# Issuing the W_in sums a step before their splits, and three smaller moves, in a fused attention and two-MLP kernel

## The chip, the cores and the metric

One core of a Trainium2 chip. The metric is the device time of one launch in microseconds (us), as a median of runs. The engines have short names in the profile: PE is TensorE (PEld its weight loads), DVE is VectorE, ACT is ScalarE, POOL is GpSimd, SP is the queue that issues the DMAs.

## The reference

```python
def _attn_ref(q, k, v, p):            # q, k, v (8, 8, 576, 64), p (8, 8, 32, 64)
    p_packed = sm_attn(p, k, v)       # softmax(p k^T / 8) v
    return sm_attn(q, p_packed, p_packed)
def _moe_ref(x, w_in, w_out):         # x (4608, 512), w_in (512, 2048), w_out (2048, 512)
    h = x @ w_in
    return (h - np.tanh(h)) @ w_out
def _moe2_ref(x, w_in, w_out):        # the same sizes
    h = x @ w_in
    return (h * np.cos(h)) @ w_out
# out = moe2(moe(attention, heads side by side))
```

## The kernel before

All large matrix products are done in a split form: a float32 operand is written as a high part, rounded to the format that TensorE takes (`hi`), and the rest (`lo`), and three products hi·hi, lo·hi and hi·lo are added in PSUM. ScalarE makes each high part, VectorE or GpSimd the low part by a subtraction.

The work stands in three stages.

**Stage A, the first MLP** (with attention worked in between): 128 steps, `n` from 0 to 127. A step takes one block of 288 tokens and 256 of the 2048 hidden columns: `h1` (12 matmuls, L454), `el1` and `el2` (tanh by two branches on ScalarE and VectorE; the choice between them is the COPY_PREDICATED of L488), `el3` (`gh`, L496) and `el4` (`gl`, L501), and two steps later `ymm1` (24 matmuls, L516), which adds to four PSUM tiles `y`. After the last step of a block `yevac1` (L552) has ScalarE copy the four tiles out, behind the `ymm1` of that step and so two steps after its `h1`. The next block's first `ymm1` writes the same four tiles. In the last 16 steps (n = 112 to 127) the weights of the second MLP are converted as well, ten of the 32 tiles. A conversion has three parts: `a` on ScalarE (L135), `b`, three VectorE instructions (L147, L152, L157) that stand between the ones of `el2` a step later, and `c`, a ScalarE copy (L180) and a GpSimd subtraction (L181), another step later. How many `a` a step gets is `STEP_A2`, indexed by n − 112.

**Stage B, the second MLP for three blocks of 512 tokens**: 24 steps, `n` from 0 to 23, in five parts (`PARTS`): tokens 0, steps of columns 0 to 3; tokens 1, columns 0 to 3; tokens 2, columns 0 to 7; tokens 0, columns 4 to 7; tokens 1, columns 4 to 7. A step is `h2` (24 matmuls, L580), the chain `el_cos` (ScalarE L602, VectorE L605, ScalarE L611 and L612, VectorE L615, ScalarE L621 which makes `gh`, VectorE L624 which makes `gl`), and then the y products of the step before (24 matmuls, L637, in `chunks`). So `gh` of step n is wanted when `h2` of step n + 1 is done. The other 22 conversions stand in steps 0 to 10. In the last steps but one of a part, `splity` splits the activations of the next part (ScalarE L568, GpSimd L569, four tiles, two a step): in steps 13, 14 for part 3 and in steps 17, 18 for part 4. From step 12 on `combine(F)` makes four sums of quarters of W_in for the third stage: six GpSimd instructions (L691, L694, four of L702), a ScalarE copy (L704), a VectorE subtraction (L705), two stores. F is 0, 1, 2, 3 in steps 12 to 15, 4 and 5 in step 16, 6 and 7 in step 17. `combine` takes two of the three buffers of the tag "st". From step 19 on `bprep` makes the activations' sums for stage C: 40 small pieces, spread over steps 19 to 23; pieces 1 and 21 are loads into "st" buffers.

**Stage C, the second MLP for the other six blocks, in three pairs**: seven products (`prod`, L783) in place of eight, from the sums. `load_wa` loads the weight sums of one F, `load_wo` those of W_out.

From step 15 of stage A on the order is written out by hand: each engine carries out its instructions in the order of the program, and waits where an operand or a buffer isn't there. A ScalarE instruction that waits holds up all that stand behind it on ScalarE. The DMAs are all issued on one queue (SP), in program order too. At the end of a step of stage B the order on ScalarE is: `gh`, the two copies of `splity`, the copies out of PSUM where a part ends, then the copy of L704; then the next step's L602.

Of the kernel before, what the change touches and what calls it, by code (L numbers as in the profile page):

```python
# [34 lines left out]
PRE_A = (0, 1, 1, 1, 1, 0, 1, 1, 1, 0, 1, 1, 0, 0, 0)  # L35
PRE_B = (1, 0, 1, 1, 2, 0, 2, 2, 0, 1, 2, 2, 0, 3, 0)
STEP_A = (1, 2, 2, 2, 1, 2, 1, 1, 1, 1, 0, 2, 1, 1, 1, 1, 1, 1, 0, 3, 1, 1)
STEP_A2 = (1, 1, 0, 1, 1, 0, 1, 1, 0, 1, 1, 0, 1, 1, 0, 0)
STEP_ORDERED = 15
ATT1 = ((-2, 0, 1, 4), (0, 1, 2, 5))  # L40
ATT = ((0, 2, 3, 8), (1, 4, 5, 10))
# [4 lines left out]
YLOAD, Y2LOAD, Y2SPLIT = 2, 118, 125  # L46
PARTS = ((0, 0, 4), (1, 0, 4), (2, 0, 8), (0, 4, 8), (1, 4, 8))
NCL, CONVS, BPREP = 3, 12, 19
COMBINE = {12: (0,), 13: (1,), 14: (2,), 15: (3,), 16: (4, 5), 17: (6, 7)}
SGN = -2147483648  # L50


# [1 line left out]
def fused_kernel(ctx, tc, qT, kT, v, pT, w1i, w1o, w2i, w2o, ident, out):  # L54
    nc = tc.nc
# [33 lines left out]
    def f32(ap):  # L89
        return ap.bitcast(F32)  # L90

    def wtile(name):
        return wp.tile([128, 2, 512], F32R, tag="w", name=name)
# [7 lines left out]
    class Conv:  # L101
# [69 lines left out]
        def b(self):  # L171
            for fn in self.b_ops():
                fn()
# [389 lines left out]
    def splity(i, yr, eng):  # L563
        if i % 2 == 0:
            t = a2p.tile([128, 2, S], F32R, tag="a2", bufs=4, name="yhl")[:, :, 0:TB]
        else:
            t = p3.tile([128, 2, TB], F32R, tag="yhl", bufs=4, name="yhl")
        nc.scalar.activation(out=t[:, 0, :], in_=yr, func=AF.Copy)  # L568
        eng.tensor_tensor(out=t[:, 1, :], in0=yr, in1=f32(t[:, 0, :]), op=ALU.subtract)  # L569
        return t  # L570

    def h2(s, yt, st):
        h = pss("h")
        for x in range(2):
            f = 2 * s + x
            conv2.need(w2in, f)
            n = 0
            for wa, ya in ((0, 0), (1, 0), (0, 1)):
                for k in range(4):
                    nc.tensor.matmul(  # L580
                        out=h[:, x, :], lhsT=w2in[f][:, wa, 128 * k:128 * k + 128],
                        rhs=yt[k][:, ya, :], start=(n == 0), stop=(n == 11),
                    )
                    n += 1
        st["h"] = h
# [100 lines left out]
    def combine(F):  # L686
        r = p2x["r"]
        f0, f1 = w2in[2 * F], w2in[2 * F + 1]
        w = r.tile([128, 2, 512], F32, tag="st", bufs=3, name="cw")
        c = r.tile([128, 4, 256], F32, tag="st", bufs=3, name="cs")  # L690
        nc.gpsimd.tensor_tensor(  # L691
            out=w[:, 0, :], in0=f32(f0[:, 0, :]), in1=f32(f0[:, 1, :]), op=ALU.add
        )
        nc.gpsimd.tensor_tensor(  # L694
            out=w[:, 1, :], in0=f32(f1[:, 0, :]), in1=f32(f1[:, 1, :]), op=ALU.add
        )
        a11, a12, a21, a22 = (w[:, i // 2, 256 * (i % 2):256 * (i % 2) + 256] for i in range(4))
        for i, (x, y, op) in enumerate((
            (a21, a22, ALU.add), (c[:, 0], a11, ALU.subtract),
            (a11, a21, ALU.subtract), (a12, c[:, 1], ALU.subtract),  # L700
        )):
            nc.gpsimd.tensor_tensor(out=c[:, i], in0=x, in1=y, op=op)  # L702
        hi, lo = (wp.tile([128, 4, 256], F32R, tag="w", name="ws") for _ in range(2))
        nc.scalar.activation(out=hi, in_=c, func=AF.Copy)  # L704
        nc.vector.tensor_tensor(out=lo, in0=c, in1=f32(hi), op=ALU.subtract)  # L705
        nc.sync.dma_start(out=wsd[F][:, 0], in_=f32(hi.rearrange("p c n -> p (c n)")))
        nc.sync.dma_start(out=wsd[F][:, 1], in_=f32(lo.rearrange("p c n -> p (c n)")))

    def load_wa(F):
        t = [wtile("wa") for _ in range(4)]  # L710
        nc.sync.dma_start(out=f32(t[2]), in_=wid[2 * F])
        for i in range(2):
            nc.sync.dma_start(out=f32(t[i].rearrange("p a n -> p (a n)")), in_=wsd[F][:, i])
        nc.sync.dma_start(out=f32(t[3][:, :, 256:512]), in_=wid[2 * F + 1][:, :, 256:512])
        sh, sl = (x.rearrange("p a n -> p (a n)") for x in t[:2])

        def combo(i):
            return [(sh, sl)[wa][:, 256 * i:256 * i + 256] for wa in range(2)]

        return {  # L720
            "S1": combo(0), "S2": combo(1), "S3": combo(2), "S4": combo(3),
            "A11": [t[2][:, wa, 0:256] for wa in range(2)],
            "A12": [t[2][:, wa, 256:512] for wa in range(2)],
            "A22": [t[3][:, wa, 256:512] for wa in range(2)],
        }
# [7 lines left out]
    def bprep(t, bo):  # L733
        ops, q = [], {}

        def split(n, j, src):
            d = bo.setdefault(n, [None, None])

            def hi():
                d[j] = wtile("b")  # L740
                nc.scalar.activation(out=d[j][:, 0, :], in_=src(), func=AF.Copy)

            def lo():
                nc.vector.tensor_tensor(
                    out=d[j][:, 1, :], in0=src(), in1=f32(d[j][:, 0, :]), op=ALU.subtract
                )

            return [hi, lo]

        def sub(o, a, b):  # L750
            return lambda: nc.vector.tensor_tensor(out=o(), in0=a(), in1=b(), op=ALU.subtract)

        for j in range(2):
            def load(j=j):
                for n, k in (("lo", j), ("hi", 2 + j)):
                    q[n, j] = p2x["r"].tile([128, 2, TB], F32, tag="st", bufs=3, name="yq")
                    nc.sync.dma_start(
                        out=q[n, j],
                        in_=y1[k, :, t * TB:t * TB + 2 * TB].rearrange("p (a n) -> p a n", a=2),
                    )  # L760

            def temp(j=j):
                q["t", j] = p2x["r"].tile([128, 2, TB], F32, tag="st", bufs=3, name="yt")

            b11, b12 = (lambda j=j, i=i: q["lo", j][:, i] for i in range(2))
            b21, b22 = (lambda j=j, i=i: q["hi", j][:, i] for i in range(2))
            t1, t2 = (lambda j=j, i=i: q["t", j][:, i] for i in range(2))
            s11, s1, s2 = split("B11", j, b11), split("T1", j, t1), split("T2", j, t2)
            s3, s21, s22 = split("T3", j, b12), split("B21", j, b21), split("B22", j, b22)
            s4 = split("T4", j, b21)  # L770
            ops += [
                load, temp, s11[0], sub(t1, b12, b11), s11[1], s1[0], sub(t2, b22, t1), s1[1],
                s2[0], sub(b12, b22, b12), s2[1], s21[0], s3[0], s21[1], sub(b21, b21, t2),
                s3[1], s22[0], s4[0], s22[1], s4[1],
            ]
        return ops
# [44 lines left out]
    def run_pool(name, **kw):  # L821
        c = tc.tile_pool(name=name, bufs=1, reuse_waits="tile", **kw)
        return c, c.__enter__()
# [140 lines left out]
    hist, yr0 = [], []  # L964
    steps = [(blk, HS * h + s) for h in range(2) for blk in range(NP) for s in range(HS)]
    steps += [(blk, s) for blk in range(NP, NB) for s in range(NSTEP)]
    for n, (blk, s) in enumerate(steps):
# [17 lines left out]
        if blk >= NB - 2:  # L985
            na = STEP_A2[n - NSTEP * (NB - 2)]
        else:
# [35 lines left out]

    p2c, p2 = run_pool("p2")
    p3c, p3 = run_pool("p3")
    pend, hist, bo, nyt = [], [], {}, []
    seq = [(i, t, s, a, b) for i, (t, a, b) in enumerate(PARTS) for s in range(a, b)]
    nxt = [p[0] for p in PARTS[1:]]

# [5 lines left out]
    for n, (i, t, s, a, b) in enumerate(seq):  # L1035
        st = {}
        if s == a and i:
            yt, nyt = nyt, []
        h2(s, yt, st)
        el_cos(st, 2 if n < CONVS else 0, n == 0)  # L1040
        if i < len(nxt):
            r = s - a - (b - a - 4)
            if r in (1, 2):
                for _ in range(2):
                    nyt.append(splity(i + 1, yr0.pop(0), nc.gpsimd))
            if r in (0, 1):
                yr0 += [loady(nxt[i], k) for k in range(2 * r, 2 * r + 2)]
        if hist:
            flush(*hist.pop(0))
            keep = 2 if n == len(seq) - 1 else 0  # L1050
            while len(pend) > keep:
                pend.pop(0)()
        hist.append((t, s, st, a, b))
        if a and s == b - 2 and n < len(seq) - 2:
            load_op(t)
        store_w2()
        for F in COMBINE.get(n, ()):
            combine(F)
        if n == BPREP:
            prep = bprep(NCL, bo)  # L1060
        if n >= BPREP:
            m = -(-len(prep) // (len(seq) - n))
            for fn in prep[:m]:
                fn()
            prep = prep[m:]
    was = [load_wa(0)]
    flush(*hist.pop(0))
    p3c.__exit__(None, None, None)
    pshc.__exit__(None, None, None)
# [17 lines left out]
    for t in pairs:  # L1087
# [66 lines left out]
        if not last:  # L1154
            bo = {}
            prep = bprep(t + 2, bo)
            was = [load_wa(0)]
        else:
            prep = []
        for F in range(NSTEP):  # L1160
# [4 lines left out]
            n = -(-len(prep) // max(1, 6 - F))  # L1165
            for fn in prep[:n]:
                fn()
            prep = prep[n:]
# [58 lines left out]
```

## Time and profile before

| what | value |
| --- | --- |
| median of 3 runs | 1590.18 us |
| lowest, highest | 1587.25, 1590.53 us |
| the profiled execution, its own time | 1587.97 us |
| span of that execution in the trace | 1586.1 us |
| PE busy | 1497.8 us, 94% |
| DVE busy | 1171.5 us, 74% |
| ACT busy | 900.2 us, 57% |
| POOL busy | 234.5 us, 15% |

Times in rows are counted from the start of the span. In the rows of stretches the first stretch is step 11 of stage B, the second its steps 12 to 19, the third the last 16 steps of stage A. By the matmuls' lines stage A ends at about 795 us, stage B runs from there to about 1078 us, and stage C from 1082 us to the end. The granted clock of TensorE (PEclk) is 1.00 at full speed.

### The profile page before, as it was taken

To read this page: it belongs to the slowest core of one execution; us is meant where nothing else is said; L and a number is where in the kernel's file an instruction comes from. 1 tells how busy PE (TensorE), PEld (TensorE's weight loads), DVE (VectorE), ACT (ScalarE), POOL (GpSimd) and SP (SyncE) were. 2 spreads that over 40 slices of the span, in tenths; PEclk is the share of its full clock that TensorE was granted. 3 is DMA by queue.
4 is the path that set the end of the run, shared out by engine and by line. 5 is a ranking of instruction groups with operands and counts; after the bars stand their busy time and mean duration, and the time that the engine had idled before them with its cause. 6 is when DMAs were issued, how large, how long until landed. Compare 5 with 4: busy or idle time off the path is not lost.

```text
span 1586.1 us, 25956 instructions
## 1 busy us (share of the span) xinstructions
PE 1497.8 (94%) x10192; PEld 1298.0 (82%) x10192; DVE 1171.5 (74%) x1604; ACT 900.2 (57%) x1385; POOL 234.5 (15%) x186
## 2 busy tenths in 40 slices
PE   4789999999999999999899998798999999999999
PEld 1669888999899999998877786687888888888887
DVE  6999988887878788789877853356777477747661
ACT  4768665675756666676656653454555354535541
POOL 3632110010101010011233327500000000000000
PEclk7789999999999999999999999999999999999999
DMA  9423322111212111114446622543757474747542
GB/s 346 152 96 105 98 79 91 64 46 31 59 51 64 61 64 61 32 53 162 136 162 230 226 100 84 196 175 129 266 188 268 147 285 162 261 157 281 189 164 116
DMA packets 88506, 223.54 MB, mean 141 GB/s; under 512 B 8960, under 2 KB 36608, under 8 KB 88384
## 3 DMA queue, kind: packets, MB, share of 16 engines
q1 hardware_dynamic: 88384, 221.88, 40.2%
q8 instruction: 81, 1.33, 0.3%
q14 instruction: 41, 0.34, 0.1%
HBM read 173.34 MB, written 48.50 MB: 140 GB/s over the span
## 4 chain that ended last, share of the span: by engine, by line
PE 68%; DVE 16%; issue 8%; POOL 4%; ACT 3%; DMA 1%; SPq 0%; DVEq 0%; POOLq 0%; ACTq 0%
PE y L516 19%; PE y L637 19%; PE p L783 15%; PE h L454 9%; DVE wt L147 2%; PE h L580 2%; DVE y L484 2%; DVE wt L157 2%; PE gp L416 2%; DVE y L488 1%; POOL cs L702 1%; DVE d L482 1%; DVE wt L152 1%; DVE t L481 1%; DVE gl L501 1%
## 5 line engine op out<-in xcount | busy, mean ns | idle before, releaser
L516 PE MATMUL y<-gh,w1o 128*128 128x288 f32 x2048 | 310.5, 304 | 11.6 <-ACT gh L496 6.7
L516 PEld LDWEIGHTS y<-gh,w1o 128*128 128x128 f32 x2048 | 283.7, 190 | 39.8 <-ACT t L469 14.9
L783 PE MATMUL p<-b,wa 128*128 128x512 f32 x1008 | 241.9, 391 | 4.1 <-issue 4.1
L454 PE MATMUL h<-a,g 128*128 128x288 f32 x1536 | 229.7, 299 | 14.0 <-ACT w1i L135 6.6
L454 PEld LDWEIGHTS h<-a,g 128*128 128x128 f32 x1536 | 214.0, 191 | 18.4 <-ACT w1i L135 7.6
L783 PEld LDWEIGHTS p<-b,wa 128*128 128x128 f32 x1008 | 190.4, 189 | 44.0 <-issue 4.5
L469 ACT ACTIVATE t<-h 128x576 f32<-128x576 f32 x128 | 83.2, 650 | 206.3 <-PE h L454 206.0
L637 PE MATMUL y<-wo,gh 128*128 128x512 f32 x768 | 188.1, 389 | 0.0
L637 PEld LDWEIGHTS y<-wo,gh 128*128 128x128 f32 x768 | 144.2, 188 | 29.9
L516 PE MATMUL y<-gl,w1o 128*128 128x288 f32 x1024 | 159.5, 298 | 1.4 <-DVE gl L501 1.4
L516 PEld LDWEIGHTS y<-gl,w1o 128*128 128x128 f32 x1024 | 145.0, 191 | 1.9 <-DVE gl L501 1.9
L580 PE MATMUL h<-yhl,w2i 128*128 128x512 f32 x576 | 134.9, 390 | 0.8 <-ACT w2i L180 0.6
L481 DVE TENSOR_TENSOR t<-h,t 128x576 f32<-128x576 f32 x128 | 95.2, 744 | 54.3 <-ACT u L470 53.9
L580 PEld LDWEIGHTS h<-yhl,w2i 128*128 128x128 f32 x576 | 108.0, 188 | 23.9 <-ACT w2i L180 1.0
L488 DVE COPY_PREDICATED y<-k,t 128x576 f32<-128x576 int16 x128 | 116.1, 907 | 11.6
L637 PE MATMUL y<-w2o,gh 128*128 128x512 f32 x384 | 99.1, 405 | 18.8 <-ACT gh L621 16.7
L794 ACT ACTIVATE a<-ha 128x1024 f32<-128x1024 f32 x24 | 25.5, 1063 | 145.6 <-DVE ha L791 145.6
L501 DVE TENSOR_TENSOR gl<-y,gh 128x576 fp32r<-128x576 f32 x128 | 102.7, 802 | 6.8 <-ACT gh L496 6.0
L496 ACT ACTIVATE gh<-y 128x576 fp32r<-128x576 f32 x128 | 87.6, 685 | 32.1 <-DVE y L488 30.1
L637 PEld LDWEIGHTS y<-w2o,gh 128*128 128x128 f32 x384 | 74.7, 196 | 37.3 <-ACT gh L621 18.7
L484 DVE SCALAR_TENSOR_TENSOR y<-y,d 128x576 f32<-128x576 f32 x128 | 101.2, 791 | 0.1
L637 PE MATMUL y<-wo,gl 128*128 128x512 f32 x384 | 97.8, 389 | 0.0
(120 smaller groups left out, 2168.4 us busy)
## 6 DMA issues: line engine op xcount, KB each, us to landing
wo<-wod SPq DMA_DIRECT2D x96, 512.0 KB, 6.6
wa<-wsd SPq DMA_DIRECT2D x48, 512.0 KB, 6.2
wa<-wid SPq DMA_DIRECT2D x24, 512.0 KB, 5.6
y<-ye SPq DMA_DIRECT2D x80, 144.0 KB, 1.9
out<-o SPq DMA_DIRECT2D x36, 256.0 KB, 2.2
st<-w1i SPq DMA_DIRECT2D x16, 512.0 KB, 7.2
v<-vv SPq DMA_DIRECT2D x16, 512.0 KB, 4.7
st<-w1o SPq DMA_DIRECT2D x16, 512.0 KB, 6.2
```

Of the source, the lines that this page charges most:

```text
L147: nc.vector.tensor_scalar(out=wi, in0=wi, scalar1=3, scalar2=None, op0=ALU.logical_shift_left)
L454: nc.tensor.matmul(out=h[:, x, 0:HB], lhsT=gw[b, f // 4, half][:, ga, c0:c0 + 128], rhs=a2[b, half][:, aa, HB * j:HB * j + HB], start=(n = ...
L469: nc.scalar.activation(out=st["t"], in_=h, func=AF.Tanh)
L481: lambda: nc.vector.tensor_tensor(out=t, in0=hs, in1=t, op=ALU.subtract),
L484: lambda: nc.vector.scalar_tensor_tensor(out=y, in0=y, scalar=PC0 - PC1 * PC1 / (4 * PC2), in1=d, op0=ALU.add, op1=ALU.mult,),
L488: lambda: nc.vector.copy_predicated(out=y, mask=k.bitcast(I16), data=t),
L496: nc.scalar.activation(out=st["gh"], in_=st["g"], func=AF.Copy)
L501: nc.vector.tensor_tensor(out=st["gl"], in0=st["g"], in1=f32(st["gh"]), op=ALU.subtract)
L516: nc.tensor.matmul(out=yps[blk][d][:, 0:HB], lhsT=w1out[f][:, wh, 128 * d:128 * d + 128], rhs=st[gg][:, x, :], start=(s in first and x == ...
L580: nc.tensor.matmul(out=h[:, x, :], lhsT=w2in[f][:, wa, 128 * k:128 * k + 128], rhs=yt[k][:, ya, :], start=(n == 0), stop=(n == 11),)
L637: nc.tensor.matmul(out=yps[t, lo_s][m], lhsT=st[gg][:, x, 128 * m:128 * m + 128], rhs=w[:, wh, :], start=(s == lo_s and x == 0 and not lo ...
L783: nc.tensor.matmul(out=dst, lhsT=wa[wi][:, 128 * j:128 * j + 128], rhs=b[j][:, bi, :], start=(n == 0), stop=(n == 5),)
```

## The change

`combine` is cut in two: `combine` issues the six GpSimd instructions, and the new `combine2` the ScalarE copy, the VectorE subtraction and the two stores, one step later. The sums are spread as 0 to 5 in steps 11 to 16 and 6 and 7 in step 17, so that `combine2` stands in steps 12 to 17 (one each) and 18 (two). The low parts of `splity` for parts 3 and 4 go from GpSimd to VectorE (eight instructions). The first piece of `bprep`, a load, stands in step 18 in place of 19, and the first `load_wa` of the pairs in step 22 in place of behind step 23. `STEP_A2` has the same ten conversions, otherwise spread: no `a` in steps 113 and 121 (the steps that end with copies out of PSUM), and the last one in step 126 in place of 125.

```diff
-STEP_A2 = (1, 1, 0, 1, 1, 0, 1, 1, 0, 1, 1, 0, 1, 1, 0, 0)
+STEP_A2 = (1, 0, 1, 1, 0, 1, 1, 0, 1, 0, 1, 1, 0, 1, 1, 0)
...
-COMBINE = {12: (0,), 13: (1,), 14: (2,), 15: (3,), 16: (4, 5), 17: (6, 7)}
+COMBINE = {11: (0,), 12: (1,), 13: (2,), 14: (3,), 15: (4,), 16: (5,), 17: (6, 7)}
...
             nc.gpsimd.tensor_tensor(out=c[:, i], in0=x, in1=y, op=op)
+        return F, c
+
+    def combine2(F, c):
         hi, lo = (wp.tile([128, 4, 256], F32R, tag="w", name="ws") for _ in range(2))
         nc.scalar.activation(out=hi, in_=c, func=AF.Copy)
         nc.vector.tensor_tensor(out=lo, in0=c, in1=f32(hi), op=ALU.subtract)
...
-    pend, hist, bo, nyt = [], [], {}, []
+    pend, hist, bo, nyt, sums = [], [], {}, [], []
...
-                    nyt.append(splity(i + 1, yr0.pop(0), nc.gpsimd))
+                    nyt.append(splity(i + 1, yr0.pop(0), nc.gpsimd if i < 2 else nc.vector))
...
-        for F in COMBINE.get(n, ()):
-            combine(F)
-        if n == BPREP:
+        for x in sums:
+            combine2(*x)
+        sums = [combine(F) for F in COMBINE.get(n, ())]
+        if n == BPREP - 1:
             prep = bprep(NCL, bo)
+            prep.pop(0)()
+        if n == len(seq) - 2:
+            was = [load_wa(0)]
         if n >= BPREP:
...
-    was = [load_wa(0)]
     flush(*hist.pop(0))
```

## Rows read from the trace of the kernel before

**Rows 1.** PE's waits, whole span: line, what ended them, us in total, times, longest
```profile
PE y L637 <- ACT gh L621: 16.7, 4, 9.4
PE p L783 <- issue: 4.1, 1, 4.1
```

**Rows 2.** Busy us (x) of PE, PEld, DVE, ACT, POOL; PEclk; DMA, by stretch
```profile
917.69:928.57 10.88, 10.88 (x49) 9.01 (x48) 6.48 (x7) 5.69 (x7) 4.92 (x4) 1.00 0.29 104
928.57:1037.81 109.24, 93.00 (x385) 75.15 (x384) 42.05 (x35) 46.72 (x51) 58.57 (x55) 0.92 0.34 125
...
698.97:795.39 96.42, 88.42 (x627) 86.58 (x625) 87.47 (x116) 65.57 (x117) 17.01 (x12) 0.96 0.42 138
```

**Rows 3.** PE in time, stage B: start, us, instructions, in brackets idle before
```profile
934.01 3.79 PE L637 MATMUL y<-w2o,gh 128*128 128x512 f32 x16
...
969.16 5.53 PE L637 MATMUL y<-w2o,gh 128*128 128x512 f32 x16 [2.35 <-ACT gh L621]
...
986.35 2.05 PE L637 MATMUL y<-w2o,gh 128*128 128x512 f32 x4 [4.40 <-ACT gh L621]
...
1030.51 5.65 PE L637 MATMUL y<-w2o,gh 128*128 128x512 f32 x16 [9.40 <-ACT gh L621]
```

**Rows 4.** ACT in time, steps 13 and 17 of stage B
```profile
945.09 1.03 ACT L602 ACTIVATE a<-h 128x1024 f32<-128x1024 f32 x1 [3.11 <-PE h L580]
...
950.85 1.06 ACT L621 ACTIVATE gh<-a 128x1024 fp32r<-128x1024 f32 x1 [1.29 <-DVE a L615]
...
961.13 1.06 ACT L704 ACTIVATE ws<-cs 128x1024 fp32r<-128x1024 f32 x1 [8.18 <-POOL cs L702]
...
1022.49 1.06 ACT L704 ACTIVATE ws<-cs 128x1024 fp32r<-128x1024 f32 x1 [5.43 <-POOL cs L702]
```

**Rows 5.** POOL in time, step 13 of stage B
```profile
952.50 3.09 POOL L569 TENSOR_TENSOR yhl<-yr,yhl 128x512 fp32r<-128x512 f32 x2 [19.74 <-ACT yhl L568]
...
960.36 0.74 POOL L702 TENSOR_TENSOR cs<-cw,cs 128x256 f32<-128x256 f32 x1
```

**Rows 6.** DVE in time: splits, `gl` beside sums on POOL, `gl` alone
```profile
793.00 1.29 DVE L569 TENSOR_TENSOR yhl<-yr,yhl 128x512 fp32r<-128x512 f32 x2 [1.28 <-ACT yhl L568]
...
986.33 2.11 DVE L624 TENSOR_TENSOR gl<-a,gh 128x1024 fp32r<-128x1024 f32 x1 [1.12 <-ACT gh L621]
...
1006.80 1.22 DVE L624 TENSOR_TENSOR gl<-a,gh 128x1024 fp32r<-128x1024 f32 x1 [1.13 <-ACT gh L621]
```

**Rows 7.** PE's waits from 670 to 800 us, columns as in Rows 1
```profile
PE y L516 <- ACT gh L496: 4.6, 3, 2.6
```

**Rows 8.** PE in time, end of stage A
```profile
753.97 3.91 PE L516 MATMUL y<-gh,w1o 128*128 128x288 f32 x16 [3.08 <-ACT ye L552]
...
763.61 1.76 PE L454 MATMUL h<-a,g 128*128 128x288 f32 x12
...
765.21 2.33 PE L516 MATMUL y<-gh,w1o 128*128 128x288 f32 x16
...
768.44 1.76 PE L454 MATMUL h<-a,g 128*128 128x288 f32 x12
```

**Rows 9.** DVE in time, steps 118 to 120 of stage A
```profile
734.99 0.74 DVE L481 TENSOR_TENSOR t<-h,t 128x576 f32<-128x576 f32 x1
...
737.83 0.83 DVE L488 COPY_PREDICATED y<-k,t 128x576 f32<-128x576 int16 x1
738.63 0.76 DVE L481 TENSOR_TENSOR t<-h,t 128x576 f32<-128x576 f32 x1
...
743.03 1.96 DVE L488 COPY_PREDICATED y<-k,t 128x576 f32<-128x576 int16 x1
744.88 0.75 DVE L481 TENSOR_TENSOR t<-h,t 128x576 f32<-128x576 f32 x1
```

**Rows 10.** ACT in time, the copies out of PSUM of step 121, stage A
```profile
753.52 1.29 ACT L552 ACTIVATE ye<-y 128x288 f32<-128x288 f32 x4
```

**Rows 11.** SP in time, the first load for the pairs
```profile
1057.52 0.42 SPq L711 DMA_DIRECT2D wa<-wid  x1
```

## The prediction

> **What bounds the kernel now.** I read PE's waits first, then the stretches in which they lie, then the queues of ScalarE, GpSimd and VectorE at those times. PE is busy for almost the whole span, so a change can gain only where PE stands still or runs slowly. The largest sum of waits that one line ends is that of the y products L637 for `gh`, 16.7 us in four waits, 9.4 the longest [rows 1]. Three of the four lie in steps 14 to 19 of stage B: 2.35, 4.40 and 9.40 us, together 16.15 [rows 3].
>
> The stretches price them. Step 11, with no sums, took 10.88 us at a granted clock of 1.00; steps 12 to 19 took 109.24 us at 0.92 [rows 2]. Eight steps of 10.88 are 87.04, so 22.20 us are lost there: 16.15 of waiting and 6.05 of slow running behind it (16 products took 5.53 and 5.65 us behind a wait, 3.79 without one [rows 3]).
>
> Why `gh` is late shows in step 13. The chain from L602 to the end of `gh` runs from 945.09 to 951.91, 6.8 us [rows 4]; a step has 10.88, so a chain may start about 4 us late before PE feels it. Then GpSimd makes two low parts of `splity` from 952.50 to 955.59 and only then the sums of F = 1, which end at 961.10, that is 5.5 us later [rows 5]. ScalarE's copy L704 idles 8.18 us for them and starts at 961.13 [rows 4], and the next step's L602 stands behind it. The same wait of 5.43 us precedes the L704 of F = 7 [rows 4]; that step pays for two splits and two sums in a row.
>
> Stage A's last 16 steps hold the second loss. A PE step without a wait is 768.44 − 763.61 = 4.83 us, one `ymm1` of it 3.23 (from 765.21) [rows 8]. Sixteen steps and the two `ymm1` that trail are 83.7 us; the stretch took 96.42 at a clock of 0.96 [rows 2], so 12.7 are lost: 4.6 in three waits for `gh` [rows 7], 3.08 for the copies out of PSUM, the rest in slow running (3.91 against 2.33 us for the 16 products behind that wait [rows 8]) and small gaps.
>
> **The change, part by part.**
>
> *Sums a step ahead, splits on VectorE.* These two go together. With the splits gone from its queue, nothing holds GpSimd in steps 12 to 18 but operands and the three "st" buffers; it idled 19.74 us ahead of the splits of step 13 [rows 5], so the room is there. Buffers: the sums of F need the VectorE subtraction of F − 2, which stands in `combine2` two program steps before the `combine2` that wants F. From that subtraction to the wanted copy is about one step, 10.9 us, and the sums need 5.5. Tightest is F = 7: its buffer comes free with the subtraction of F = 5 at the end of step 17, about 10 us behind the end of `h2`; its sums end about 5.5 us later, 4.6 us into step 18, and the copy is wanted about 9 us in. That leaves over 4 us. So L704 no longer waits, and ScalarE carries per step a chain of 6.8 us and one or two copies of 1.06 [rows 4], with two split copies at the most: about 10 of 10.88 us in step 18.
>
> VectorE takes two low parts in each of four steps, 1.29 us the pair [rows 6], behind `gl` and so off the chain. The worst step is 18: chain 6.8, `gl` 1.22 [rows 6], splits 1.29, two subtractions of the size of `gl`, 2.4; that ends 11.7 us behind `h2`, while the next L605 could start at 10.88 + 1.03 = 11.9 [rows 2, 4]. What is queued behind the splits on VectorE is the subtraction L705 and the next chain, which has the 4 us. What the trace does not show is VectorE's splits beside sums on GpSimd. The nearest row is `gl`: 2.11 us beside GpSimd, 1.22 alone [rows 6]. The bounds are nothing, and 0.89 on each of up to five instructions, 4.5 us in step 18 and less elsewhere; against the 4 us of cover, 0 to 3 us in all reach PE. A gain below the 10.88 of a clean step is excluded, since PE has no gap there. I take 0.5 us, since `gl` and the subtractions lie behind `gh`, and L605 and L615, which make it, read PSUM and show no such lengthening in the chain above. Stage B: 22.2 − 0.5 = **21.7 us**.
>
> A rule of the Trainium skill speaks against this part (SBUF — State Buffer, "Who interferes with whom"): a VectorE instruction with two SBUF inputs and a GpSimd instruction that reads SBUF exclude each other, and the second waits until the first is finished. The `gl` row agrees in kind. By the rule each of four or five such instructions would wait out one GpSimd instruction; the second rival prices that from rows.
>
> *`STEP_A2`.* A plain step costs VectorE 738.63 − 734.99 = 3.64 us, a step with conversion 744.88 − 738.63 = 6.25 [rows 9]. Against PE's 4.83 the first gives back 1.19 and the second puts VectorE 1.42 behind. By step 120 the old order has six conversions and two plain steps since the first (steps 113 to 120): 8.5 − 2.4 = 6.1 us behind. There PE waits 3.08 [rows 8], for the copies of step 121, which start at 753.52 [rows 10] because ScalarE's `gh` and a conversion's copy stand in front of them. So about 3 us of lag are free. The new order has five conversions and three plain steps up to 120: 7.1 − 3.6 = 3.5, about 0.5 beyond what is free, and no conversion's copy in step 121: the wait of 3.08 goes, with its slow running. Over all steps both orders end 10 × 1.42 − 5 × 1.19 = 8.25 behind, the old one after a peak of 9.4. So what is late next are the last steps: two conversions now stand in steps 126 and 127.
>
> Bounds of what is left: at 6.25 a conversion, 8.25 − 3 = 5.3 us of waits, against 7.7 now; at 5.12 (L488 takes 1.96 beside a GpSimd subtraction and 0.83 alone [rows 9], so 1.13 less) only 0.29 is added per conversion and nothing waits. The gain lies between 2.4 and 12.7 us. I take **7.5**, the middle: VectorE lags less up to step 121, so the copy `c` runs less far ahead and meets L488 less often, but the end is fuller. The tenth conversion's `c` moves into step 0 of stage B, ahead of its first chain: 0 to 1.06 us (L704, a copy of twice its size [rows 4]); I take 0.3.
>
> *`bprep`'s first load and `load_wa` sooner.* Costed at nothing. SP is past the first `load_wa` at 1057.52 [rows 11], while the first product of stage C starts only behind 1078: the load had some 20 us already, so it was not what PE waited for. The wait of 4.1 us at that product [rows 1] has no releaser in the trace; I leave it, with 0 to 4.1 as its bounds. `bprep`'s load is queued on SP behind the four stores of step 18, which wait for the two subtractions; nothing behind it on SP is wanted before step 20. If these stores were late, ScalarE's first `bprep` copy would wait for the load, behind `gh` of step 19 and with 4 us of cover. One `bprep` piece fewer in the last step is worth under 1 us.
>
> **Sum.** 21.7 + 7.5 − 0.3 = 28.9 us off the profiled execution's 1587.97 gives 1559.1. The median shown is 2.2 above that execution, the lowest run 0.7 below it. I say 1560 us.
>
> **The rivals.**
>
> *The wait of stage A only moves.* The conversions are as many as before and VectorE is what falls behind. For it: both orders end 8.25 behind. Against: the copies of step 121, the one wait not on `gh`, lie before the end. Stage A gains 0 to 2.4: 1566 to 1568.
>
> *GpSimd and VectorE hold each other up.* Each GpSimd instruction that meets one of VectorE with two SBUF operands delays it by up to its own length, about 1.5 us (half of the two splits' 3.09 [rows 5]), and is itself delayed. Five meetings in a split step are 7.5 us against 4 of cover: 3.5 in each of the four split steps, 14 at the worst, half of it likely. For it: the 2.11 row. Against: it is 0.89, not 1.5, and the chain's own instructions are free of it. 1564 to 1572. The page named above is the rule behind this one.
>
> *The sums don't start sooner.* If the three "st" buffers and not the splits hold GpSimd, the sums of 6 and 7 still end late and the wait of 9.40 with its slow running, 11.3 us, stays: 1570 to 1571. Against: the sums of step 13 follow the splits without a gap [rows 5].
>
> *Slower.* If a VectorE instruction must wait for the whole group of six sums (5.5 us) rather than for one of them, `gl`, the subtraction and the splits wait up to three times a step, 16.5 us. From about 8 us a step on (4 of cover, and 4 × 8 = 32 against the gain of 29) the change loses; at 16.5 it gives about 100 − 29 = 71 us more, 1659. The place is steps 12 to 18, at `gl`. Against: `gl` beside sums took 2.11.
>
> **How the numbers follow.** Forecast 0.60; wait moves 0.18; engines hold each other up 0.12; sums not sooner 0.05; slower 0.03; and 0.02 that the parts cancel. The forecast's own bounds are 1590.5 − 19 − 2.4 = 1569 and 1587.3 − 22.2 − 11 = 1554. I widen to 1553 to 1573 for the second and third rival. A measurement of this kernel tells about 0.2% (3 us) from no change. Faster by more 0.95, same 0.02, slower 0.03.
>
> **What would show it.** Stage B's steps 12 to 19 at 87 to 90 us and a clock near 1.00; L704 without a wait for GpSimd; `h2` and the y products alternating without gaps. L569 on VectorE at 0.7 to 1.5 us. In stage A no wait of L516 for the copies L552, the 16 steps at 86 to 92 us, and what waits remain in the last three steps. Stage C the same length to 1 us. The prediction is wrong if L602 waits for VectorE's `gl` in steps 13 to 19, if the stretch of stage A is still over 94 us, or if stage C is longer because a load comes late.

## The result, and the profile after

The changed kernel takes 1562.01 us (median of four runs, 1561.58 to 1562.63); the kernel before, run beside it, 1589.74 (1587.25 to 1590.53). The ratio is 0.9828, with a 95% interval of 0.9811 to 0.9846. The forecast was 1560, the range 1553 to 1573. The profiled execution took 1562.27, its span 1560.5.

Lines below L702 moved by three: L707 is the copy L704 of before, L708 the subtraction L705, L786 the product L783.

The first view is that of the stretches: us, then busy us (x instructions) of PE, PEld, DVE, ACT and POOL, then PEclk and DMA. The three rows are the last 16 steps of stage A, step 11 of stage B, and its steps 12 to 19.

```profile
700.77:791.55 90.78, 86.59 (x627) 85.11 (x625) 83.06 (x116) 65.06 (x117) 14.96 (x11) 0.98 0.43 140
914.24:925.12 10.88, 10.88 (x50) 9.01 (x48) 6.34 (x7) 5.55 (x7) 4.93 (x4) 1.00 0.27 99
925.12:1012.16 87.04, 87.04 (x386) 72.10 (x384) 44.52 (x43) 46.42 (x50) 41.86 (x47) 1.00 0.41 147
```

Against [rows 2], steps 12 to 19 lost 22.20 us: they last exactly eight steps of 10.88, PE is busy throughout and the clock is 1.00. The 16 steps of stage A lost 5.64. The account of the span (1586.1 to 1560.5, 25.6 less) closes with three more pieces: the stretch between these two is 0.39 longer (133.18 to 133.57), what lies ahead of the 16 steps 1.80 longer (698.97 to 700.77), and the rest is equal to 0.1. The code ahead of the 16 steps is the same; in the runs below that stretch took 698.2 to 701.1, so the 1.80 is no effect of the change.

PE's waits from 680 us on (line, what ended them, us in total, times, longest us):

```profile
PE p L786 <- issue: 4.1, 1, 4.1
PE y L516 <- ACT gh L496: 4.0, 3, 2.7
...
PE y L637 <- ACT gh L621: 1.1, 1, 1.1
```

Of the 16.7 us for `gh` in [rows 1] only 1.1 is left, in step 0 of stage B. ScalarE in time (start, us, instruction, in brackets idle before), steps 13 and 18:

```profile
948.36 1.14 ACT L568 ACTIVATE yhl<-yr 128x512 fp32r<-128x512 f32 x2
949.40 1.04 ACT L707 ACTIVATE ws<-cs 128x1024 fp32r<-128x1024 f32 x1
952.52 1.03 ACT L602 ACTIVATE a<-h 128x1024 f32<-128x1024 f32 x1 [2.07 <-PE h L580]
...
1003.80 1.99 ACT L707 ACTIVATE ws<-cs 128x1024 fp32r<-128x1024 f32 x2
1006.92 1.03 ACT L602 ACTIVATE a<-h 128x1024 f32<-128x1024 f32 x1 [1.12 <-PE h L580]
```

The copy that idled 8.18 us for GpSimd in [rows 4] follows the splits without a gap, and the next chain's L602 waits for PE, as it should. VectorE in steps 13 and 19, and GpSimd's sums of F = 2 and, in the last row, F = 3:

```profile
942.70 1.22 DVE L605 SCALAR_TENSOR_TENSOR a<-a,h 128x1024 f32<-128x1024 f32 x1 [2.72 <-ACT a L602]
...
949.63 1.28 DVE L569 TENSOR_TENSOR yhl<-yr,yhl 128x512 fp32r<-128x512 f32 x2
950.83 1.22 DVE L708 TENSOR_TENSOR ws<-cs,ws 128x1024 fp32r<-128x1024 f32 x1
...
1007.98 1.22 DVE L605 SCALAR_TENSOR_TENSOR a<-a,h 128x1024 f32<-128x1024 f32 x1 [0.39 <-ACT a L602]
```
```profile
940.12 0.73 POOL L702 TENSOR_TENSOR cs<-cw 128x256 f32<-128x256 f32 x1 [2.65 <-DVE ws L708]
...
943.14 1.28 POOL L691 TENSOR_TENSOR cw<-w2i 128x512 f32<-128x512 f32 x1
```

The pair of splits costs 1.28, as alone in [rows 6] (1.29). GpSimd's second half of the sums starts when VectorE's L708 has freed the "st" buffer, that is, when VectorE is through with its step. So in steps 12 to 18 no `gl`, split or subtraction of VectorE's meets a sum. Only the first sums, issued in step 11, meet a `gl`: it takes 1.29 us in place of 1.22, and one of GpSimd's, otherwise 0.74, takes 1.71. L605 does run beside sums, as at 942.70, and keeps its 1.22. The 0.39 is all that VectorE had left when step 19 began.

What is left of waiting at the end of stage A, and the first product of stage C, on PE:

```profile
747.24 2.43 PE L516 MATMUL y<-gh,w1o 128*128 128x288 f32 x16 [1.11 <-ACT gh L496]
...
783.12 3.88 PE L516 MATMUL y<-gh,w1o 128*128 128x288 f32 x16 [2.68 <-ACT gh L496]
...
1056.31 5.97 PE L786 MATMUL p<-b,wa 128*128 128x512 f32 x18 [4.10 <-issue]
```

### The profile page after: what moved, and what is told of

Read it like the earlier page. It is cut to its first block, busy times and chain, and to the rows that moved or that the text cites. A ratio compares the mean times of both kernels' runs of the same rounds, so it can differ in the third digit from the quotient of the medians.

```text
span 1560.5 us, 25954 instructions
## 1 busy us (share of the span) xinstructions
PE 1492.4 (96%) x10192; PEld 1295.9 (83%) x10192; DVE 1171.1 (75%) x1612; ACT 900.4 (58%) x1385; POOL 217.1 (14%) x178
## 4 chain that ended last, share of the span: by engine, by line
PE 74%; DVE 14%; issue 7%; ACT 2%; DMA 2%; POOL 1%; SPq 0%; DVEq 0%; ACTq 0%; POOLq 0%
PE y L637 22%; PE y L516 19%; PE p L786 15%; PE h L454 9%; PE h L580 5%; DVE wt L147 2%; DVE wt L157 1%; PE gp L416 1%; DVE y L484 1%; DVE wt L152 1%; DMA st<-w1i 1%; DVE d L482 1%; DVE y L488 1%; DVE t L481 1%; DVE gl L624 1%
## 5 line engine op out<-in xcount | busy, mean ns | idle before, releaser
L516 PE MATMUL y<-gh,w1o 128*128 128x288 f32 x2048 | 310.3, 303 | 7.8 <-ACT gh L496 7.8
L516 PEld LDWEIGHTS y<-gh,w1o 128*128 128x128 f32 x2048 | 283.8, 190 | 35.5 <-ACT t L469 14.9
L786 PE MATMUL p<-b,wa 128*128 128x512 f32 x1008 | 241.9, 391 | 4.1 <-issue 4.1
L786 PEld LDWEIGHTS p<-b,wa 128*128 128x128 f32 x1008 | 190.3, 189 | 44.1 <-issue 4.5
L516 PE MATMUL y<-gl,w1o 128*128 128x288 f32 x1024 | 159.3, 298 | 1.4 <-DVE gl L501 1.4
L516 PEld LDWEIGHTS y<-gl,w1o 128*128 128x128 f32 x1024 | 144.8, 190 | 1.9 <-DVE gl L501 1.9
L481 DVE TENSOR_TENSOR t<-h,t 128x576 f32<-128x576 f32 x128 | 95.2, 744 | 53.7 <-ACT u L470 53.2
L488 DVE COPY_PREDICATED y<-k,t 128x576 f32<-128x576 int16 x128 | 112.9, 882 | 11.6
L637 PE MATMUL y<-w2o,gh 128*128 128x512 f32 x384 | 94.4, 390 | 3.2 <-DVE o L680 2.0
L482 DVE TENSOR_TENSOR d<-u,h 128x576 f32<-128x576 f32 x128 | 94.9, 742 | 0.0
```

Source lines behind the costliest of these rows:

```text
L481: lambda: nc.vector.tensor_tensor(out=t, in0=hs, in1=t, op=ALU.subtract),
L482: lambda: nc.vector.tensor_tensor(out=d, in0=u, in1=hs, op=ALU.mult),
L488: lambda: nc.vector.copy_predicated(out=y, mask=k.bitcast(I16), data=t),
L516: nc.tensor.matmul(out=yps[blk][d][:, 0:HB], lhsT=w1out[f][:, wh, 128 * d:128 * d + 128], rhs=st[gg][:, x, :], start=(s in first and x == ...
L637: nc.tensor.matmul(out=yps[t, lo_s][m], lhsT=st[gg][:, x, 128 * m:128 * m + 128], rhs=w[:, wh, :], start=(s == lo_s and x == 0 and not lo ...
L786: nc.tensor.matmul(out=dst, lhsT=wa[wi][:, 128 * j:128 * j + 128], rhs=b[j][:, bi, :], start=(n == 0), stop=(n == 5),)
```

## The experiments

Times stand against the kernel before on the same chip: 1589.92 us beside the first four, 1590.21 beside the next four, 1589.37 beside the last three. The first five are the kernel before with one or two parts of the change, the others the changed kernel with an edit.

**Which part removes the 22 us?**

> The kernel before with one part alone: the low parts of the y splits for parts 3 and 4 on VectorE. Theory A (the splits hold the sums up in GpSimd's queue, so moving them is enough): steps 12 to 19 of stage B in 87 to 89 us in place of 109, all of the 22 us gained, about 1567.5 us. Theory B (the sums must be issued a step ahead, since in the kernel before ScalarE's copy stands in the same step as the sums): at least the step with F = 6 and 7 still waits, 9.4 us of wait plus slow running stay, about 1578 us. Stage A as before in both.

```diff
-                    nyt.append(splity(i + 1, yr0.pop(0), nc.gpsimd))
+                    nyt.append(splity(i + 1, yr0.pop(0), nc.gpsimd if i < 2 else nc.vector))
```

1566.53 us (1564.95 to 1568.12), ratio 0.9857 (0.9839 to 0.9875): Theory A. The stretch of steps 12 to 19, then a row of ScalarE and two of VectorE in step 17:

```profile
928.61:1015.65 87.04, 87.04 (x386) 72.10 (x384) 46.17 (x43) 46.42 (x50) 44.66 (x47) 1.00 0.43 157
```
```profile
999.66 1.06 ACT L704 ACTIVATE ws<-cs 128x1024 fp32r<-128x1024 f32 x1 [2.20 <-POOL cs L702]
```
```profile
996.64 2.38 DVE L569 TENSOR_TENSOR yhl<-yr,yhl 128x512 fp32r<-128x512 f32 x2
998.95 3.03 DVE L705 TENSOR_TENSOR ws<-cs,ws 128x1024 fp32r<-128x1024 f32 x2
```

The eight splits alone give all of it. The sums are still issued in the step that wants them: a copy waits 2.20 us, and VectorE's splits and subtractions beside sums take 2.38 and 3.03 in place of 1.28 and 2.35. PE notices none of it, since the next L602 stands at 1000.63, about 1 us late, inside the 4 us of cover.

> The kernel before with one part alone: sums issued a step ahead of their copies and spread as 0 to 5 in steps 11 to 16, 6 and 7 in step 17; the y splits stay on GpSimd. Theory A (the splits are what holds the sums): GpSimd still carries splits, but a step of slack now stands between the sums and the copy, so most of the gain comes too; what is late next is the split of step 18 itself, queued behind the sums of 6 and 7, and the first product of part 4 waits about 2 us for it: 1569 to 1571 us. Theory B (only the step ahead counts): the full 22 us, about 1567.5 us, with no wait at step 20.

```diff
-COMBINE = {12: (0,), 13: (1,), 14: (2,), 15: (3,), 16: (4, 5), 17: (6, 7)}
+COMBINE = {11: (0,), 12: (1,), 13: (2,), 14: (3,), 15: (4,), 16: (5,), 17: (6, 7)}
...
+        return F, c
+
+    def combine2(F, c):
...
-        for F in COMBINE.get(n, ()):
-            combine(F)
+        for x in sums:
+            combine2(*x)
+        sums = [combine(F) for F in COMBINE.get(n, ())]
```

1567.71 us (1567.06 to 1569.18), ratio 0.9864 (0.9849 to 0.9878). The same stretch, and the late copy of step 18:

```profile
930.15:1017.19 87.04, 87.04 (x386) 72.10 (x384) 41.84 (x34) 44.30 (x48) 61.33 (x55) 1.00 0.38 136
```
```profile
1014.63 1.06 ACT L707 ACTIVATE ws<-cs 128x1024 fp32r<-128x1024 f32 x1 [4.75 <-POOL cs L702]
1015.60 1.01 ACT L602 ACTIVATE a<-h 128x1024 f32<-128x1024 f32 x1
```

This part alone gives all of it too. The expected 2 us of waiting in step 20 for a split on GpSimd did not come: the time is Theory B's. But the cover is used up: the chain of step 19 starts at 1015.60, about 3.7 us late, and its `gh` ends at 1022.62 (1021.56 + 1.06), just as PE turns to it at 1022.67; `gl` comes too late and step 20 takes 11.45. So the two parts are redundant here: either clears the queue in front of ScalarE's copy, and both together leave more room, not more time.

**The other parts.**

> The kernel before with one part alone: the other spread of the ten conversions over the last 16 steps of stage A. Theory (VectorE's lag, and the copies out of PSUM queued on ScalarE behind a late high part): those 16 steps in about 91 us in place of 96.4, no wait for the copies, 5 to 6 us gained, 1584 us. Rival (the wait only moves): under 2 us gained, 1588 us or more.

```diff
-STEP_A2 = (1, 1, 0, 1, 1, 0, 1, 1, 0, 1, 1, 0, 1, 1, 0, 0)
+STEP_A2 = (1, 0, 1, 1, 0, 1, 1, 0, 1, 0, 1, 1, 0, 1, 1, 0)
```

1584.72 us (1584.13 to 1586.55), ratio 0.9972 (0.9960 to 0.9983): 5.2 us. The 16 steps of stage A:

```profile
699.62:790.48 90.86, 86.59 (x626) 85.08 (x625) 83.13 (x116) 65.12 (x116) 14.96 (x11) 0.98 0.43 140
```

The wait for the copies L552 is gone and three waits for `gh`, 4.0 us, remain, as in the whole change. The old order is less steady than the new one: in the four traces that have it (before, splits alone, sums alone, loads alone) the 16 steps took 95.38 to 97.47 us, in the six with the new one and no other edit there 90.75 to 90.86.

> The kernel before with one part alone: the first load of the pairs' activations one step and the first weight load of the pairs two steps sooner in program order. Theory (no engine waits for them): no difference, 1590 us within 1.5, and the wait of 4.1 us at the first product of stage C unchanged. Rival (that wait is for a load): the 4.1 us go, 1586 us.

```diff
-        if n == BPREP:
+        if n == BPREP - 1:
             prep = bprep(NCL, bo)
+            prep.pop(0)()
+        if n == len(seq) - 2:
+            was = [load_wa(0)]
...
-    was = [load_wa(0)]
```

1589.94 us (1587.92 to 1592.48), ratio 1.0002 (0.9992 to 1.0011): nothing. PE's wait behind 1040 us is the one of before, 4.1 us at L783 [rows 1].

> The kernel before with two parts of the change: splits on VectorE and the new spread of conversions. The sums stay in the step of their copies, and the loads where they were. Theory (in stage B either the splits' move or the step ahead is enough alone, because a chain may be 4 us late before TensorE feels it): the same as the whole change, 1561.5 us within 1.5. Rival (the step ahead adds something once stage A is shorter): 1563.5 us or more.

The two edits of the first and the third run together: 1561.92 us (1559.90 to 1562.67), ratio 0.9822 (0.9806 to 0.9837). The two stretches:

```profile
701.14:791.94 90.80, 86.62 (x627) 85.15 (x625) 83.02 (x116) 65.06 (x117) 14.94 (x11) 0.98 0.43 140
925.54:1012.58 87.04, 87.04 (x385) 72.07 (x384) 46.15 (x43) 46.41 (x50) 44.60 (x47) 1.00 0.43 157
```

23.4 and 5.2 us alone, 28.3 together: the gains add up, and these two edits are the whole change as far as it can be measured.

**What holds the end of stage A?**

> The changed kernel with GpSimd's subtraction of the first ten conversions (L181) on VectorE. Theory (L488 is long because GpSimd's subtraction and it exclude each other): all L488 at about 0.83 us; VectorE loses about 6 us of such waiting and gains ten instructions of 0.6 us, so the 16 steps of stage A stay at 89 to 91.5 us and the kernel at 1561 to 1563. Rival (L488 is long for a reason of its own): five L488 stay at 1.9 us, the 16 steps grow to 94 us or more.

```diff
...
-            nc.gpsimd.tensor_tensor(out=t[:, 1, :], in0=w, in1=f32(t[:, 0, :]), op=ALU.subtract)
+            (nc.vector if self.cvec and self.nc_ < 10 else nc.gpsimd).tensor_tensor(
+                out=t[:, 1, :], in0=w, in1=f32(t[:, 0, :]), op=ALU.subtract
+            )
...
```

1559.58 us (1558.65 to 1561.30), ratio 0.9810 (0.9795 to 0.9826). The 16 steps, PE's two waits for `gh` in them (L520 is L516), and the one COPY_PREDICATED that is still long (L492 is L488):

```profile
698.21:786.40 88.19, 84.51 (x626) 83.52 (x625) 81.97 (x125) 65.51 (x117) 3.18 (x2) 1.00 0.43 144
```
```profile
777.33 2.44 PE L520 MATMUL y<-gh,w1o 128*128 128x288 f32 x16 [1.55 <-ACT gh L500]
...
783.07 2.43 PE L520 MATMUL y<-gh,w1o 128*128 128x288 f32 x16 [1.62 <-ACT gh L500]
```
```profile
769.28 1.76 DVE L492 COPY_PREDICATED y<-k,t 128x576 f32<-128x576 int16 x1
```

The stretch is 2.6 us shorter than in the changed kernel, a little more than expected, although VectorE has nine instructions more in it: a low part costs it 0.68 us, a COPY_PREDICATED beside GpSimd's subtraction cost 1.1 more. Fifteen of the 16 COPY_PREDICATED take 0.80 to 0.85; the sixteenth takes 1.76 beside the two splits of step 125, which are still on GpSimd. Only the next run, with less work, has a lower ratio; the interval of this run overlaps that of the change, so that it beats it is likely, not settled.

> The changed kernel without the second VectorE instruction (L152, the sign) of the conversions in stage A: that part of the computation is left out, so VectorE carries ten instructions of 0.6 us less there and nothing else changes. Theory (the waits left at the end of stage A are VectorE's lag): at most 1 us of waits for the high parts, the 16 steps at 84.5 to 87 us in place of 90.8, the kernel at 1556 to 1558. Rival (they come from ScalarE's queue or from the buffers): the 16 steps stay at 89 us or more.

```diff
...
-            return [shift, low] if sgn is not None else [shift, sign, low]
+            return [shift, low] if sgn is not None or (self.skip and f < 5) else [shift, sign, low]
...
```

1556.27 us (1554.53 to 1558.01), ratio 0.9788 (0.9772 to 0.9805). The 16 steps, then VectorE and GpSimd where they meet in step 124 (L489 is L488, L182 is L181):

```profile
700.46:785.63 85.17, 83.96 (x627) 83.45 (x626) 75.08 (x106) 64.47 (x117) 15.37 (x11) 1.00 0.46 149
```
```profile
765.99 0.84 DVE L489 COPY_PREDICATED y<-k,t 128x576 f32<-128x576 int16 x1
```
```profile
766.52 1.44 POOL L182 TENSOR_TENSOR w2o<-wt,w2o 128x512 fp32r<-128x512 f32 x1 [3.52 <-ACT w2o L181]
```

Ten instructions of 0.68 us, 6.8 together, take 5.61 us off the stretch: VectorE's time is what is waited for. And though GpSimd has all its subtractions, every COPY_PREDICATED takes 0.81 to 0.85: VectorE, no longer late, has begun it when the subtraction comes, and GpSimd waits instead (about 1.45 us against 1.30). The meetings themselves don't end: L147 (L148 here), 0.42 us elsewhere, takes 0.86 to 1.48 in five steps.

**Stage C's first product.**

> The changed kernel with no y products kept back at the last step of stage B (before, two of the three parts were kept for later gaps). Theory (the 4.1 us at the first product of stage C are a wait for VectorE's last reading of the PSUM tile that the product overwrites): the two parts, 3.6 us of products, fill that gap, the wait falls to about 0.5 us, 1558.5 us. Rival (the parts are missed behind the first three products, where new gaps open): 1561 to 1562 us, with waits at the second group of products.

```diff
-            keep = 2 if n == len(seq) - 1 else 0
+            keep = 0
```

1561.92 us (1560.96 to 1565.65), ratio 0.9830 (0.9808 to 0.9852). PE's waits from 1040 us on:

```profile
PE y L637 <- ACT gh L818: 2.8, 1, 2.8
PE p L786 <- PE y L637: 0.5, 1, 0.5
```

The gap of 4.10 is filled, but the first product starts at 1056.18, as in the changed kernel (1056.31), and the expected 3.5 us are not there. In both it follows VectorE's last reading of PSUM, L615, by 0.10 us (1054.86 + 1.22 here, 1054.99 + 1.22 there). It does so in the traces of the first, second and fourth run and of the kernel before too; where L615 ended later, with the sums alone, the wait was 4.7. No run moved L615 by itself, so that it is the cause is read from these times. The two pieces of y products that now fill the gap are missing at the end of the first pair, where a new wait of 2.8 us stands: the rival had the time right and expected the place right behind the first products.

**GpSimd beside VectorE, and the cover.**

> The changed kernel with the sums' result in a buffer of the large pool in place of one of the three st buffers, so that GpSimd needn't wait for VectorE's subtraction two sums before and runs its 48 instructions in a row. Theory (GpSimd and VectorE exclude each other on two-operand instructions, but the 4 us of cover hide it): gl, the splits and the subtractions of steps 12 to 15 that meet a sum take 0.5 to 1.3 us longer, and no time is lost: 1562 us within 1.5. Rival (the buffers were what kept the sums clear of VectorE, and without them the two hold each other up beyond the cover): waits of L637 for gh in steps 13 to 16, 1565 us or more.

```diff
-        c = r.tile([128, 4, 256], F32, tag="st", bufs=3, name="cs")
+        c = wp.tile([128, 4, 256], F32, tag="w", name="cs")
```

1561.01 us (1559.77 to 1561.93), ratio 0.9823 (0.9807 to 0.9839). The stretch, and VectorE in step 13 beside sums that now run in a row:

```profile
923.33:1010.37 87.04, 87.04 (x386) 72.10 (x385) 51.97 (x43) 46.42 (x50) 50.98 (x47) 1.00 0.41 147
```
```profile
946.70 1.72 DVE L624 TENSOR_TENSOR gl<-a,gh 128x1024 fp32r<-128x1024 f32 x1 [1.13 <-ACT gh L621]
948.34 2.93 DVE L569 TENSOR_TENSOR yhl<-yr,yhl 128x512 fp32r<-128x512 f32 x2
951.20 1.76 DVE L708 TENSOR_TENSOR ws<-cs,ws 128x1024 fp32r<-128x1024 f32 x1
```

With the gate gone the engines do meet: 0.50 us on `gl`, 1.65 on the pair of splits, 0.54 on the subtraction, 2.7 in one step. In step 14 it is 3.1 (`gl` 1.57, splits 2.93, subtraction 2.31), the next L605 stands behind them, and that chain's `gh` ends at 970.98, 1.3 us before PE wants it at 972.28. The chain's L602, L605 and L615 keep their lengths, and PE loses nothing. The rule of the Trainium skill (SBUF — State Buffer, "Who interferes with whom") that the second waits until the first is finished agrees in kind; each meeting costs a part of an instruction, and the cover pays it.

> The changed kernel with useless copies on ScalarE behind gh: five more in step 12, nine more in step 15 of stage B, 0.97 us each. Theory (a chain may start about 4 us late before TensorE waits: 10.88 less 6.85): the chain of step 13 starts 1.9 us late and TensorE does not wait; the chain of step 16 starts 5.6 us late and TensorE waits 1.6 us, once, with up to 2 us of slow running behind: 1563.5 to 1566 us. Rival (the cover is half of that): 0 and 3.6 us of wait, 1566 us or more; or none at all in both, 1562 us.

```diff
...
-        nc.scalar.activation(out=hi, in_=c, func=AF.Copy)
+        for _ in range(1 + dose):
+            nc.scalar.activation(out=hi, in_=c, func=AF.Copy)
...
-            combine2(*x)
+            combine2(*x, {12: 5, 15: 9}.get(n, 0))
```

1566.97 us (1565.99 to 1568.87), ratio 0.9861 (0.9847 to 0.9876). The stretch, ScalarE in steps 13, 15 and 16, and PE behind it:

```profile
923.19:1016.82 93.63, 90.23 (x386) 74.11 (x384) 44.32 (x43) 60.80 (x64) 41.85 (x47) 0.96 0.38 136
```
```profile
941.96 1.01 ACT L602 ACTIVATE a<-h 128x1024 f32<-128x1024 f32 x1
...
968.18 10.88 ACT L708 ACTIVATE ws<-cs 128x1024 fp32r<-128x1024 f32 x10
978.97 1.01 ACT L602 ACTIVATE a<-h 128x1024 f32<-128x1024 f32 x1
...
984.99 1.06 ACT L621 ACTIVATE gh<-a 128x1024 fp32r<-128x1024 f32 x1 [1.29 <-DVE a L615]
985.95 1.06 ACT L678 ACTIVATE o<-y 128x512 f32<-128x512 f32 x2
```
```profile
986.59 6.80 PE L637 MATMUL y<-w2o,gh 128*128 128x512 f32 x16 [3.40 <-ACT o L678]
```

Five extra copies in step 12 make the next chain about 2.4 us late (`h2` ended at 939.51): no wait. Nine in step 15 put L602 6.8 us behind the end of `h2` (972.15): `gh` ends at 986.05, 2.9 after PE is done with the next `h2`. So the cover is about 4 us, as worked out ahead of the change. The y products wait 3.40, since they want the first copy out of PSUM (L678) too, which stands behind `gh` here. The wait brings 16 products of 6.80 instead of 3.79: 3.40 + 3.01 of the 6.59 us that the stretch is longer. The time lies about 1 us above what was expected, in the range of the rival, and the wait is near the rival's 3.6; but half the cover, about 2 us, would have made the chain that starts 2.4 late wait, and the one that starts 6.8 late wait 4.8 for `gh`. The difference to the expected time comes from the copies, which take 1.08 in a row and not 0.97, from L678, and from slow running that is worth as much as the wait.

**The edits together.**

> The changed kernel with the first ten low parts of the weights and the two splits of step 125 on VectorE, and one y product part kept back at the last step of stage B in place of two. Theory (each was seen or costed alone: low parts 2.4 us; the splits keep GpSimd off VectorE at the end of stage A, up to 1 us; one more part fills half of the 4.1 us at stage C's first product, of which the end of the first pair gives back some, 1 us): 1557 to 1559 us. Rival (only the low parts count): 1559.5 us or more.

```diff
...
-            yt = [splity(0, yr0.pop(0), nc.gpsimd) for k in range(2)]
+            yt = [splity(0, yr0.pop(0), nc.vector) for k in range(2)]
...
-            keep = 2 if n == len(seq) - 1 else 0
+            keep = 1 if n == len(seq) - 1 else 0
```

With the low parts on VectorE as well: 1559.45 us (1558.98 to 1561.91), ratio 0.9816 (0.9801 to 0.9830). Two of PE's waits behind 690 us:

```profile
PE p L790 <- issue: 2.3, 1, 2.3
...
PE y L641 <- ACT gh L822: 1.3, 1, 1.3
```

No better than the low parts alone. One piece kept halves the first wait and brings half of the second. The splits on VectorE bring nothing that can be seen: every COPY_PREDICATED is short now, but the waits for `gh` at the end of stage A are 1.43 and 1.62 in place of 1.55 and 1.62, and the stretch took 89.54 us in place of 88.19, because the 16 products behind the second wait took 3.92 in place of 2.43.

## Why the prediction was right, point by point

In sum 28.9 us were forecast; the two profiles show 25.6, the medians 27.7. Of the 3.3 between forecast and profiles 1.9 are those of stage A's last 16 steps and 1.8 lie ahead of them, where the code is the same; the 0.5 set aside for GpSimd goes the other way.

**Stage B, 21.7 predicted, 22.2 measured.** The mechanism was right in each step that could be seen: L707 without a wait, L569 at 1.28, L602 waiting for PE alone, a clean step of 10.88 eight times. The sums of F = 7 end at 998.66 and the two copies of the step begin at 1003.80, F = 7's as the second: over 5 us to spare, where over 4 were predicted. VectorE's step 18 was said to end 0.2 us ahead of the next L605; it was 0.39. What the prediction did not see is that the two edits it priced together are each enough. It took them for one part, so it could not be wrong about the time, only about what is needed.

**The 0.5 us for GpSimd beside VectorE.** Zero reached PE, for two reasons: the "st" buffers keep the engines apart in the changed kernel, which the prediction did not see, and where they meet (the run with the sums ungated) the cover takes it, which it did. One reading of the prediction does not carry what rests on it: the chain of step 13, where L605 and L615 "show no such lengthening", ran while GpSimd was idle (its 19.74 us end at 952.50 [rows 5]). The point itself holds, as L605 at 942.70 beside a sum shows.

**`STEP_A2`, 7.5 predicted, 5.6 in the profile, 5.2 in its own run.** This is the term that was mis-sized, inside its bounds of 2.4 and 12.7. The wait for the copies went, and most of what is left stands at the end, as said: 2.68 us of wait and 1.55 of slow running (3.88 against 2.33 in [rows 8]). Another 1.11 stands at the products of step 119, not in the last three steps that the prediction named, though it had put 0.5 us beyond the free lag at step 120. The figure before is in part luck: by the traces above the old order costs 4.5 to 6.7 us more than the new one. (The range's lower end takes 11 us for this term, where 12.7 was worked out as its bound.) The failed step is the sum of lags, "both orders end 10 × 1.42 − 5 × 1.19 = 8.25 behind". VectorE doesn't add up its lag over all steps: at step 123 it has none, L481 starts at 758.79 and ScalarE's `u` ended at 758.76. What is late at the end comes from the last steps. VectorE's rows of step 126 in the changed kernel, GpSimd's beside them, and ScalarE's `gh` of step 124:

```profile
775.45 0.76 DVE L481 TENSOR_TENSOR t<-h,t 128x576 f32<-128x576 f32 x1 [1.00 <-ACT u L470]
776.12 1.00 DVE L147 TENSOR_SCALAR wt<-wt 128x512 int32<-128x512 int32 x1
...
780.43 1.92 DVE L488 COPY_PREDICATED y<-k,t 128x576 f32<-128x576 int16 x1
```
```profile
780.40 1.29 POOL L181 TENSOR_TENSOR w2i<-wt,w2i 128x512 fp32r<-128x512 f32 x1 [3.56 <-ACT w2i L180]
```
```profile
770.90 0.69 ACT L496 ACTIVATE gh<-y 128x576 fp32r<-128x576 f32 x1 [2.10 <-DVE y L488]
```

At 775.45 VectorE waits for ScalarE. ScalarE is late in its turn, since its `gh` at 770.90 had waited 2.10 us for the L488 of step 124, 1.96 long beside GpSimd, and the two copies of the splits stand behind that `gh`: a lag of VectorE's goes on through ScalarE's queue. Along VectorE's rows of step 126 the 2.68 us of PE add up as 1.00 of idling for ScalarE's `u`, 0.58 more for L147 (0.42 in seven of its ten) beside the splits on GpSimd, and 1.09 more for L488 beside the low part, 2.67 in all. None of the three was tried apart. The run with the low parts on VectorE agrees with the last: there the instruction takes 0.80 in this step and the wait is 1.55, 1.13 less (the next product then waits 1.62, where slow running had covered it); but the idling is gone there as well, and the COPY_PREDICATED of the step before takes 1.76. L488 took 1.9 us in five of the 16 steps, before in eight, so the low price of a conversion held for half of them.

**`c` in step 0, 0.3 predicted:** the stretch from stage B's start to step 12 is 0.39 longer, and PE's wait for `gh` in step 0 is longer by 0.5 us: 1.11 or 1.12 in the six traces with the new order and 0.58 to 0.60 in the four with the old.

**Loads, nothing predicted:** nothing, and the 4.1 us ahead of stage C stayed. The prediction left this wait open; by the times it ends with VectorE's L615, and not with a load.

**The rivals.** The wait of stage A that only moves is refuted by the 5.2 us of its own run, though a part of what was lost did move to the end. That the engines hold each other up is true and hidden. That the sums don't start sooner is half true: the "st" buffers hold GpSimd for 2.65 to 6.51 us ahead of the sums' second half, but issued a step ahead they still end in time. The group of six that holds up VectorE did not occur: beside sums in a row the worst row was 2.93 for two instructions.

## What to carry to other kernels

Where a helper engine's result is wanted by an engine that also carries the critical chain, look first for what stands ahead of it in the helper's own queue; here taking that out and issuing the work sooner were each enough. Work out the cover of a step (its length less the chain's) before pricing contention: what delays work behind the chain costs nothing up to there, and beyond it can count more than once, as a wait and as slow running behind it (here 22.2 us for 16.15 of waiting, and 6.59 for 3.40). Don't add up lags over steps without looking whether the engine catches up in between.

## What was not expected of the hardware

The meeting of GpSimd and VectorE depends on who is late. The same COPY_PREDICATED took 1.92 to 1.96 us when VectorE lagged and met the subtraction already begun (by 0.03 us at 780.43), and 0.81 to 0.85 in all steps of the run in which VectorE kept up, where GpSimd's subtraction took about 1.45 instead. So a small lag feeds itself: with 6.8 us of VectorE's work removed no COPY_PREDICATED was lengthened any more.

Slow running behind a wait is not fixed by the wait: 16 products behind 2.68 us took 3.88 us, behind 1.62 us 2.43, behind 3.40 us 6.80 (there of 512 columns, 3.79 without a wait). It is not fixed by the code either. With the splits alone and with the sums alone stage A is the same, and so is the wait for its last but one `gh`:

```profile
788.35 2.44 PE L516 MATMUL y<-gh,w1o 128*128 128x288 f32 x16 [2.65 <-ACT gh L496]
```
```profile
788.17 4.21 PE L516 MATMUL y<-gh,w1o 128*128 128x288 f32 x16 [2.65 <-ACT gh L496]
```

The granted clock over these 16 products was 1.00 in the first and 0.50 in the second, the lower of TensorE's two levels (1.2 in place of 2.4 GHz). So up to 1.8 us of a stretch's time can differ between two traces of the same code.
